# Zero rows, a placement table, warm-up products and moved loads in a kernel of linear attention followed by two dense layers

## The chip, the cores and the metric

The kernel runs on one core of a Trainium2 chip. The metric is the device time of one execution in microseconds (us). Times are given as the median over the runs of a kernel, with the lowest and highest in brackets. Where a profile is read, "span" is the profiled core's time from first to last recorded work, a little shorter than the device time.

## The reference

```python
# q, k, v, o_gate: (4, 8, 768, 40); i_gate, f_gate: (4, 8, 768)
for t in range(S):
    m_new = np.maximum(f_gate[:, :, t] + m, i_gate[:, :, t])
    f_stab = np.exp(f_gate[:, :, t] + m - m_new)
    i_stab = np.exp(i_gate[:, :, t] - m_new)
    C = f_stab * C + i_stab * outer(v_t, k_t)          # 40 x 40 state
    n = f_stab * n + i_stab * k_t
    y[t] = sigmoid(o_gate[t]) * (C @ q_t) / np.maximum(np.abs(n @ q_t), 1.0)
x = y.transpose(0, 2, 1, 3).reshape(3072, 320)
h = np.maximum(x @ w_in, 0.0)                            # w_in: 320 x 2048
out = (s * (h * h) + b) @ w_out                          # w_out: 2048 x 320
```

With gates as large as these, only the first 42 time steps still weigh in the state at later times. The kernel uses 42 rows of k and v for each head, checks on the chip that this was allowed (the "flag" steps), and holds a full version that isn't run with these inputs.

## The kernel before

The 3072 tokens go through in six chunks of 512. A chunk has four rounds of products for the two dense layers, and the attention of the *next* chunk is spread over sixteen slots between them, 0 to 15. Chunks 0 to 3 hold most of one batch each. Chunks 4 and 5 hold the first and last 128 tokens of every batch and need more steps.

```python
# one chunk, in the order in which PE gets its work
at = self.events(c + 1) if c + 1 < 6 else {}
for k in range(4):
    self.mm1_rem(c, k, 0); self.mm1_rem(c, k, 1)       # remainder products, 64 rows
    for a in range(2):
        self.mm1(c, k, a)                              # main products of layer 1
        self.square(*prev)                             # VectorE, of the half round before
        self.relu(c, k, a)                             # ScalarE
        for n, (f0, f1) in enumerate((((0, 3), (3, 6)), ((6, 11), (11, 16)))[a]):
            for e in at.get(4 * k + 2 * a + n, []):    # slot
                e()
            self.mm2(c - 1, k, f0, f1)                 # layer 2 of the chunk before
```

The attention operands have 42 rows, and one transpose buffer in PSUM (`psT`, one deep) serves nearly every attention step:

```python
self.kp = c.tile([L, B, 9, D], BF16, name="kp")        # L = 42
self.v1 = c.tile([L, B, 9, D + 1], BF16, name="v1")
self.psT = ctx.enter_context(tc.tile_pool(name="psT", bufs=1, space=PSUM))
...
def ev_vr(self, bb):
    ps = self.psT.tile([3 * L, 3, 3, D + 1], F32, tag="t", name="ps_vr")
    for g in range(3):
        nc.tensor.matmul(ps[:, g, :, :], lhsT=self.sel..., rhs=self.v1[:, bb, 3 * g : 3 * g + 3, :], ...)
    nc.vector.tensor_tensor(out=vbd, in0=ps, in1=self.bdl..., op=ALU.mult)
```

`ev_q` transposes the queries (`ps_q`), `ev_cn` builds the state (`ps_cn`), `ev_h` multiplies queries by state (`ps_h`) and starts a chain of five VectorE operations that ends in `x`. `ev_x` transposes `x` (`ps_x`) into the input `xt` of the layers. `ev_kt` and `ev_vr` make `kbd` and `vbd` for chunks 4 and 5, `ev_s` makes scores (`ps_s`) and `pm`. `warm(n)` issues n products of ones that nobody reads. They keep the matrix engine's clock up.

## Time and profile before

| kernel before | value |
|---|---|
| median of 3 runs | 161.21 us (161.01 to 161.81) |
| profiled run | 161.73 us, span 160.0 us, mean granted clock 0.972 |
| PE / VectorE / ScalarE busy | 89% / 55% / 49% of the span |

PE is the matrix engine, DVE is VectorE, ACT is ScalarE. The list of waits of PE gives the engine and tile, what ended the wait, the total in us, the number of times and the longest one:

```profile
PE o L424 <- DVE osb L430: 2.9, 3, 1.0
PE hp L380 <- ACT xt L366: 2.9, 3, 1.1
PE ps_q L290 <- ACT qb L275: 1.9, 2, 0.9
```

The first and the third line are holes in chunks 1, 3 and 4, where PE is the bound: 4.8 us that a better placement could close. The second stands in chunk 0 and at the opening of chunk 1, where products of the first layer wait for their transposed input.

### The profile page before, as it was taken

Reading aid. Unit: us, or ns where it says so; the run is one execution under the profiler, and the core shown is the slowest. Engines: PE = TensorE matmul, PEld = TensorE weight load, DVE = VectorE, ACT = ScalarE, POOL = GpSimd, SP = SyncE. Lnnn points to the kernel's source line nnn. Section 1 sums busy time; section 2 is a strip of 40 time slices with the busy share of each in tenths; the row PEclk is TensorE's granted clock in tenths of the full one; section 3 lists DMA queues with packets and bytes.
Section 4 is the critical chain, followed back from the end, with each engine's and each line's share of the span. In section 5 each row is a group of like instructions: output and inputs, shape, how many; then the busy total and the mean of one; then the engine's idle time right before and its main releaser. Section 6 shows DMA issues by size and latency. Waiting matters only on the chain.

```text
span 160.0 us, 2702 instructions
## 1 busy us (share of the span) xinstructions
PE 141.6 (89%) x1053; PEld 83.1 (52%) x1067; DVE 88.6 (55%) x188; ACT 78.7 (49%) x92; POOL 20.4 (13%) x48
## 2 busy tenths in 40 slices
PE   7896799889999799999979997979998899999970
PEld 7674443346555445665445563535544554556750
DVE  1486379951496665867436668335695444344220
ACT  4242468735674548855484454474725543533000
POOL 7974975000000000000000000000000000000000
PEclk9998589999999999999999999999999999999997
DMA  3999999920590110169501049610010111110221
GB/s 70 313 173 272 248 169 167 310 85 0 148 259 9 41 41 2 49 134 194 124 0 45 0 99 198 117 41 26 15 43 4 41 41 41 41 45 11 78 82 53
DMA packets 32265, 15.32 MB, mean 96 GB/s; under 512 B 20596, under 2 KB 31668, under 8 KB 32244
## 3 DMA queue, kind: packets, MB, share of 16 engines
q1 hardware_dynamic: 27000, 9.71, 25.0%
q0 software_dynamic: 4544, 5.24, 16.3%
q8 instruction: 10, 0.16, 0.5%
q10 hardware_dynamic: 700, 0.11, 0.4%
q14 instruction: 11, 0.09, 0.2%
HBM read 13.75 MB, written 3.93 MB: 110 GB/s over the span
## 4 chain that ended last, share of the span: by engine, by line
PE 62%; DVE 13%; DMA 10%; ACT 4%; issue 4%; POOL 4%; POOLq 0%; DVEq 0%; ACTq 0%
PE o L424 22%; PE hp L392 21%; DMA wi<-in_moe_w_in_dram 9%; PE o2t L424 5%; PE hp L380 5%; DVE fac L347 3%; DVE x L352 3%; PE ps_q L290 2%; DVE osb L430 2%; ACT xt L366 2%; PE ps_h L324 2%; ACT r L399 1%; PE ps_b L412 1%; PE ps_x L364 1%; DMA out_dram<-osb 1%
## 5 line engine op out<-in xcount | busy, mean ns | idle before, releaser
L399 ACT ACTIVATE r<-hp 128x1024 bf16<-128x1024 f32 x48 | 49.2, 1024 | 56.8 <-PE hp L392 56.0
L424 PE MATMUL o<-wo,g 128*128 128x320 bf16 x320 | 53.0, 299 | 3.2 <-DVE osb L430 2.9
L392 PE MATMUL hp<-xt,wi 128*128 128x512 bf16 (+1 forms) x186 | 48.1, 379 | 1.7 <-issue 1.1
L424 PEld LDWEIGHTS <-g 128*128 128x128 bf16 x384 | 35.5, 98 | 19.4 <-issue 4.5
L406 DVE TENSOR_TENSOR g<-r 128x1024 bf16<-128x1024 bf16 x48 | 32.1, 682 | 9.4 <-ACT r L399 9.3
L392 PEld LDWEIGHTS <-wi 128*128 128x128 bf16 x200 | 17.4, 99 | 23.7 <-issue 10.4
L430 DVE SCALAR_TENSOR_TENSOR osb<-o,sc,brep 128x320 f32<-128x320 f32 x20 | 11.0, 548 | 16.4 <-PE o L424 16.3
L380 PE MATMUL hp<-xt,wr 64*128 64x512 bf16 (+1 forms) x100 | 16.4, 382 | 3.3 <-ACT xt L366 2.9
L366 ACT COPY xt<-ps_x 128x768 bf16<-128x768 bf16 x12 | 9.5, 794 | 5.0 <-PE ps_x L364 5.0
L347 DVE SCALAR_TENSOR_TENSOR fac<-th,rec 128x640 f32<-128x640 f32 x12 | 9.9, 824 | 0.6
L352 DVE TENSOR_TENSOR x<-ps_h,fac 128x640 bf16<-128x640 f32 x12 | 9.9, 824 | 0.4
L380 PEld LDWEIGHTS <-wr 64*128 64x128 bf16 x100 | 3.9, 95 | 9.9 <-issue 7.9
L424 PE MATMUL o2t<-wo,g 128*128 128x320 bf16 x64 | 8.9, 299 | 0.0
L490 PE MATMUL ps_w<-ones 128*128 128x128 bf16 x96 | 7.8, 249 | 1.1 <-POOL ones L131 1.1
L290 PE MATMUL ps_q<-idb,qb 128*128 128x128 bf16 x72 | 6.2, 227 | 2.7 <-ACT qb L275 1.9
L290 PEld LDWEIGHTS <-qb 128*128 128x128 bf16 x72 | 5.0, 102 | 5.0 <-ACT qb L275 2.6
L490 PEld LDWEIGHTS <-ones 128*128 128x128 bf16 x96 | 7.0, 115 | 1.2 <-POOL ones L131 1.1
L293 ACT COPY qt<-ps_q 128x768 bf16<-128x768 bf16 x9 | 7.2, 797 | 0.6 <-PE ps_q L290 0.6
L364 PE MATMUL ps_x<-idb,x 128*128 128x128 bf16 x72 | 6.6, 227 | 0.8 <-DVE x L352 0.2
L364 PEld LDWEIGHTS <-x 128*128 128x128 bf16 x72 | 5.2, 102 | 4.0 <-DVE x L352 1.3
L281 ACT ACTIVATE th<-ox 128x640 f32<-128x640 f32 x8 | 5.8, 733 | 0.3 <-DMA ox<-in_o_gate_dram 0.3
L430 DVE SCALAR_TENSOR_TENSOR osb<-o2t,sc,brep 128x320 f32<-128x320 f32 x4 | 2.2, 550 | 5.9 <-PE o2t L424 5.9
(90 smaller groups left out, 88.0 us busy)
## 6 DMA issues: line engine op xcount, KB each, us to landing
out_dram<-osb SPq DMA_DIRECT2D x24, 160.0 KB, 2.4
qx<-in_q_dram SPq DMA_DIRECT2D x2, 640.0 KB
ox<-in_o_gate_dram SPq DMA_DIRECT2D x2, 640.0 KB
qx<-in_q_dram POOLq DMA_DIRECT2D x2, 640.0 KB, 9.9
ox<-in_o_gate_dram POOLq DMA_DIRECT2D x2, 640.0 KB, 10.9
wo<-in_moe_w_out_dram POOLq DMA_DIRECT2D x4, 320.0 KB, 7.0
qy<-in_q_dram SPq DMA_DIRECT2D x8, 160.0 KB, 3.2
oy<-in_o_gate_dram SPq DMA_DIRECT2D x8, 160.0 KB, 3.7
```

The lines of the kernel that those rows point to most:

```text
L290: nc.tensor.transpose(ps[:, j, g, :], self.qb[:, t0 + j, g * 120 : g * 120 + P], self.idb[:])
L347: nc.vector.scalar_tensor_tensor(out=fac, in0=self.th.pop((c, i))[:, :, :, :].rearrange("p j h d -> p (j h) d"), scalar=1.0, in1=rec[:, :] ...
L352: nc.vector.tensor_tensor(out=x[:, :, 0:DM].rearrange("p j (h d) -> p j h d", h=H), in0=hv[:, :, :, 0:D], in1=fac[:, :, :].rearrange("p (j ...
L364: nc.tensor.transpose(ps[:, j, kt, :], x[:, j, kt * P : (kt + 1) * P], self.idb[:])
L366: nc.scalar.copy(out=self.xt[:, :, t0 : t0 + 2 * P].rearrange("p k (j t) -> p j k t", j=2), in_=ps)
L380: nc.tensor.matmul(hp[:, e, n0:n1], lhsT=self.wr[64 * e : 64 * e + 64, k, a * P : (a + 1) * P], rhs=self.xt[64 * e : 64 * e + 64, 2, t0 + ...
L392: nc.tensor.matmul(hp[:, e, n0:n1], lhsT=self.wi[:, kt, f * P : (f + 1) * P], rhs=self.xt[:, kt, t0 + n0 : t0 + n1], start=False, stop=(kt ...
L399: self.nc.scalar.activation(out=r1, in_=self.hp.pop((c, k, a)), func=ACT.Relu)
L406: self.nc.vector.tensor_tensor(out=self.g[c][:, f : f + 3 : 2, :], in0=r1, in1=r1, op=ALU.mult)
L424: nc.tensor.matmul(self.o2[c, tb][:], lhsT=self.g[c][:, f, tb * P : (tb + 1) * P], rhs=self.wo[:, f, :], start=(f == 0), stop=(f == NF - 1),)
L430: nc.vector.scalar_tensor_tensor(out=osb, in0=self.o2.pop((c, tb)), scalar=self.sc[:, 0:1], in1=self.brep, op0=ALU.mult, op1=ALU.add)
L490: self.nc.tensor.matmul(self.ps_w[:, 0:P], lhsT=self.ones[:], rhs=self.ones[:], start=True, stop=True)
```

## The change

Its intent is to make PE's small products as cheap as large ones, to hold PE's clock during the start, and to put every attention step where PE doesn't wait for it. Cut to its core:

```diff
-        self.kp = c.tile([L, B, 9, D], BF16, name="kp")
-        nc.gpsimd.memset(self.kp[:, :, 8, :], 0.0)
+        self.kp = c.tile([P, B, 9, D], BF16, name="kp")        # P = 128
+        nc.vector.memset(self.kp, 0.0)
+        self.v1 = c.tile([P, B, 9, D + 1], BF16, name="v1")
+        nc.vector.memset(self.v1, 0.0)
...  # tri42, sel, ps_kt likewise; kbd, vbd 2 -> 4 buffers, r1 3 -> 4
-        self.warm(6)
+        self.warm(10)
...  # 12 -> 16, 8 -> 12, 36 -> 40, and two new warm(14) in chunk 0
+    def load_rest2(self):                                       # fa, ia: now after k, v; issued in chunk 1
...
-    def events(self, c):
+    def events(self):
+        put(0, 3, self.ev_q, 1, 1, v)                           # before: slot 4
+        put(0, 4, self.ev_h, 1, 0)                              # 5
+        put(0, 8, self.ev_x, 1, 0)                              # 9
+        put(0, 8, self.ev_h, 1, 1)                              # 10
+        put(0, 12, self.ev_x, 1, 1)                             # 14
+        put(0, 13, self.make_tri)                               # 11
+        # chunk 1: (q0, t0, e0, h0, q1, t1, e1, x0, h1, x1)
+        (3, 4, 5, 8, 5, 8, 7, 10, 12, 14)
+        put(1, 6, self.ev_kt, 0); put(1, 9, self.ev_vr, 0)      # before: all eight
+        put(1, 11, self.ev_kt, 1); put(1, 13, self.ev_vr, 1)    #   ps_kt and ps_vr
+        put(2, 12, self.ev_kt, 2); put(2, 13, self.ev_vr, 2)    #   in chunks 3 and 4
+        put(2, 14, self.ev_kt, 3); put(2, 15, self.ev_vr, 3)
+        for c in (4, 5):                                        # d = c - 1
+            put(d - 1, 13, self.qcast, c, 0, a)                 # a chunk earlier
...  # flag steps from chunks 1 and 2 to 2 and 3; loads of y about eight slots earlier
-            nc.sync.dma_start(out=dst, in_=osb)
+            eng = nc.scalar if (c, tb) == (5, CT - 1) else nc.sync
+            eng.dma_start(out=dst, in_=osb)
```

More of the change, by code (lines that the diff above doesn't have):

```diff
@@ L86, in load_rest @@
         nc.sync.dma_start(out=self.bc, in_=d["b"].partition_broadcast(P))
+        self.load_kv(2, B, nc.sync)
+    def load_rest2(self):
+        nc, d = self.nc, self.d
         nc.sync.dma_start(out=self.fa, in_=d["f"].rearrange("b h (a s) -> (b h a) s", a=4))
         nc.sync.dma_start(out=self.ia, in_=d["i"].rearrange("b h (a s) -> (b h a) s", a=4))
-        self.load_kv(2, B, nc.sync)
     def load_kv(self, b0, b1, eng):
@@ L148, in masks @@
             )
-        self.kp = c.tile([L, B, 9, D], BF16, name="kp")
-        nc.gpsimd.memset(self.kp[:, :, 8, :], 0.0)
-        self.v1 = c.tile([L, B, 9, D + 1], BF16, name="v1")
-        nc.gpsimd.memset(self.v1[:, :, 0:H, D : D + 1], 1.0)
-        nc.gpsimd.memset(self.v1[:, :, H, :], 0.0)
+        self.kp = c.tile([P, B, 9, D], BF16, name="kp")
+        nc.vector.memset(self.kp, 0.0)
+        self.v1 = c.tile([P, B, 9, D + 1], BF16, name="v1")
+        nc.vector.memset(self.v1, 0.0)
+        nc.gpsimd.memset(self.v1[0:L, :, 0:H, D : D + 1], 1.0)
         self.qb = c.tile([P, 6 * CT, 368], BF16, name="qb")
@@ L161, in masks_late @@
         nc, c = self.nc, self.const
-        self.tri42 = c.tile([L, P], BF16, name="tri42")
+        self.tri42 = c.tile([P, P], BF16, name="tri42")
         nc.gpsimd.memset(self.tri42, 1.0)
@@ L167, in masks_late @@
         )
-        self.sel = c.tile([L, 3, L], BF16, name="sel")
-        nc.gpsimd.tensor_copy(out=self.sel, in_=self.idb[0:L, 0:L].unsqueeze(1).to_broadcast([L, 3, L]))
+        self.sel = c.tile([P, 3, L], BF16, name="sel")
+        nc.gpsimd.tensor_copy(out=self.sel, in_=self.idb[:, 0:L].unsqueeze(1).to_broadcast([P, 3, L]))
         nc.gpsimd.memset(self.ib2[:, :, 1:2], 2.0)
@@ L207, in kw @@
         nc.vector.tensor_tensor(
-            out=self.kp[:, bb, 0:H, :],
+            out=self.kp[0:L, bb, 0:H, :],
             in0=self.k32[:, bb * H : (bb + 1) * H, :],
@@ L214, in vw @@
     def vw(self, bb):
-        self.nc.gpsimd.tensor_copy(out=self.v1[:, bb, 0:H, 0:D], in_=self.v32[:, bb * H : (bb + 1) * H, :])
+        self.nc.gpsimd.tensor_copy(out=self.v1[0:L, bb, 0:H, 0:D], in_=self.v32[:, bb * H : (bb + 1) * H, :])
     def ev_cn(self, bb):
@@ L233, in ev_kt @@
         nc = self.nc
-        ps = self.psT.tile([3 * D, 3, L], BF16, tag="t", name="ps_kt")
+        ps = self.psT.tile([3 * D, 3, P], BF16, tag="t", name="ps_kt")
         for g in range(3):
             nc.tensor.transpose(
-                ps[:, g, :], self.kp[:, bb, 3 * g : 3 * g + 3, :].rearrange("k a m -> k (a m)"), self.idb[0:L, 0:L]
+                ps[:, g, :], self.kp[:, bb, 3 * g : 3 * g + 3, :].rearrange("k a m -> k (a m)"), self.idb[:]
             )
-        kbd = self.kbd[bb] = self.work.tile([3 * D, 3, 3, L], BF16, tag="kbd", bufs=2, name="kbd")
+        kbd = self.kbd[bb] = self.work.tile([3 * D, 3, 3, L], BF16, tag="kbd", bufs=B, name="kbd")
         nc.vector.tensor_tensor(
             out=kbd,
-            in0=ps[:, :, :].unsqueeze(2).to_broadcast([3 * D, 3, 3, L]),
+            in0=ps[:, :, 0:L].unsqueeze(2).to_broadcast([3 * D, 3, 3, L]),
             in1=self.bdm[0 : 3 * D, :].unsqueeze(1).unsqueeze(3).to_broadcast([3 * D, 3, 3, L]),
@@ L254, in ev_vr @@
             )
-        vbd = self.vbd[bb] = self.work.tile([3 * L, 3, 3, D + 1], BF16, tag="vbd", bufs=2, name="vbd")
+        vbd = self.vbd[bb] = self.work.tile([3 * L, 3, 3, D + 1], BF16, tag="vbd", bufs=B, name="vbd")
         nc.vector.tensor_tensor(
@@ L397, in relu @@
     def relu(self, c, k, a):
-        r1 = self.r1[c, k, a] = self.work.tile([P, 2, N], BF16, tag="r1", name="r1")
+        r1 = self.r1[c, k, a] = self.work.tile([P, 2, N], BF16, tag="r1", bufs=4, name="r1")
         self.nc.scalar.activation(out=r1, in_=self.hp.pop((c, k, a)), func=ACT.Relu)
@@ L490, in warm @@
             self.nc.tensor.matmul(self.ps_w[:, 0:P], lhsT=self.ones[:], rhs=self.ones[:], start=True, stop=True)
-    def events(self, c):
-        if c == 1:
-            return {
-                0: [lambda: self.kw(1), lambda: self.qcast(1, 0, self.nc.vector)], 1: [lambda: self.ev_cn(1)],
-                2: [lambda: self.ev_q(1, 0, self.nc.vector), lambda: self.qcast(1, 1, self.nc.vector)],
-                3: [lambda: self.tanh(1, 0)], 4: [lambda: self.ev_q(1, 1, self.nc.vector)],
-                5: [lambda: self.ev_h(1, 0)], 6: [lambda: self.tanh(1, 1)], 9: [lambda: self.ev_x(1, 0)],
-                10: [lambda: self.ev_h(1, 1)], 14: [lambda: self.ev_x(1, 1)],
-            }
-        e = {}
-        def put(at, *steps):
-            for n, step in zip(at, steps):
-                e.setdefault(n, []).append(step)
-        late = 2 if c == 2 else 0
-        for i in range(2):
-            n = late + 3 * i
-            put((n, n + 1), lambda i=i: self.qcast(c, i, self.nc.scalar), lambda i=i: self.tanh(c, i))
-        if c < B:
-            put(
-                (0, 1, 2 + late, 4 + late, 5 + late, 8 + late, 9 + late, 13 + late // 2), lambda: self.kw(c),
-                lambda: self.ev_cn(c), lambda: self.ev_q(c, 0), lambda: self.ev_h(c, 0), lambda: self.ev_q(c, 1),
-                lambda: self.ev_x(c, 0), lambda: self.ev_h(c, 1), lambda: self.ev_x(c, 1),
-            )
-            return e
-        for i, at in enumerate(((0, 1, 3, 4, 6, 10), (2, 5, 7, 8, 11, 14))):
-            bb, _ = self.pair(c, i)
-            put(
-                at, lambda bb=bb: self.ev_kt(bb), lambda i=i: self.ev_q(c, i), lambda bb=bb: self.ev_vr(bb),
-                lambda i=i: self.ev_s(c, i), lambda i=i: self.ev_h(c, i), lambda i=i: self.ev_x(c, i),
-            )
@@ new lines, in events, with put @@
+    def events(self):
+        e = {}
+        def put(c, at, step, *args):
+            e.setdefault((c, at), []).append(lambda: step(*args))
+        v, a = self.nc.vector, self.nc.scalar
+        put(0, 0, self.kw, 1)
+        put(0, 0, self.qcast, 1, 0, v)
+        put(0, 1, self.ev_cn, 1)
+        put(0, 1, self.qcast, 1, 1, v)
+        put(0, 2, self.ev_q, 1, 0, v)
+        put(0, 3, self.tanh, 1, 0)
+        put(0, 3, self.ev_q, 1, 1, v)
+        put(0, 4, self.ev_h, 1, 0)
+        put(0, 5, self.tanh, 1, 1)
+        put(0, 8, self.ev_x, 1, 0)
+        put(0, 8, self.ev_h, 1, 1)
+        put(0, 12, self.ev_x, 1, 1)
+        put(0, 13, self.make_tri)
+        put(1, 3, self.bias)
+        put(1, 3, self.load_rest2)
+        for c in (2, 3):
+            q0, t0, e0, h0, q1, t1, e1, x0, h1, x1 = (
+                (3, 4, 5, 8, 5, 8, 7, 10, 12, 14) if c == 2 else (0, 1, 2, 4, 3, 4, 5, 7, 8, 11)
+            )
+            d = c - 1
+            put(d, 0, self.kw, c)
+            put(d, 1, self.ev_cn, c)
+            put(d, q0, self.qcast, c, 0, a)
+            put(d, t0, self.tanh, c, 0)
+            put(d, e0, self.ev_q, c, 0)
+            put(d, h0, self.ev_h, c, 0)
+            put(d, q1, self.qcast, c, 1, a)
+            put(d, t1, self.tanh, c, 1)
+            put(d, e1, self.ev_q, c, 1)
+            put(d, x0, self.ev_x, c, 0)
+            put(d, h1, self.ev_h, c, 1)
+            put(d, x1, self.ev_x, c, 1)
+        put(1, 6, self.ev_kt, 0)
+        put(1, 9, self.ev_vr, 0)
+        put(1, 11, self.ev_kt, 1)
+        put(1, 13, self.ev_vr, 1)
+        put(2, 12, self.ev_kt, 2)
+        put(2, 13, self.ev_vr, 2)
+        put(2, 14, self.ev_kt, 3)
+        put(2, 15, self.ev_vr, 3)
+        for c in (4, 5):
+            d = c - 1
+            put(d - 1, 13, self.qcast, c, 0, a)
+            put(d, 0, self.ev_q, c, 0)
+            put(d, 1, self.qcast, c, 1, a)
+            put(d, 1, self.tanh, c, 0)
+            put(d, 2, self.ev_s, c, 0)
+            put(d, 3, self.ev_q, c, 1)
+            put(d, 3, self.tanh, c, 1)
+            put(d, 4, self.ev_h, c, 0)
+            put(d, 5, self.ev_s, c, 1)
+            put(d, 7, self.ev_x, c, 0)
+            put(d, 8, self.ev_h, c, 1)
+            put(d, 11, self.ev_x, c, 1)
+        put(1, 4, self.load_x, 3, self.nc.sync)
+        put(1, 15, self.load_y, 0, self.nc.sync)
+        put(2, 15, self.load_y, 2, self.nc.sync)
+        put(2, 1, self.flag_a)
+        put(2, 5, self.flag_b)
+        put(2, 9, self.flag_c)
+        put(3, 9, self.flag_d)
@@ L553, in start @@
         self.qcast(0, 1, nc.scalar)
-        self.warm(12)
+        self.warm(16)
         self.ev_q(0, 0)
         self.ev_q(0, 1, nc.vector, early=True)
-        self.warm(8)
+        self.warm(12)
         self.tanh(0, 0)
@@ L561, in start @@
         self.ev_h(0, 1, early=True)
-        self.warm(36)
+        self.warm(40)
         self.ev_x(0, 0)
+        self.warm(14)
     def run(self):
@@ L569, in run @@
             prev = None
-            extra = {
-                (0, 2): self.make_tri, (1, 0): lambda: self.load_x(3, nc.sync), (1, 1): self.flag_a,
-                (1, 2): self.flag_b, (1, 3): self.flag_c, (2, 0): self.flag_d,
-                (2, 1): lambda: self.load_y(0, nc.sync), (3, 1): lambda: self.load_y(2, nc.sync),
-            }
+            at = self.events()
             for c in range(6):
-                at = self.events(c + 1) if c + 1 < 6 else {}
                 for k in range(4):
@@ L586, in run @@
                         self.ev_x(0, 1)
+                        self.warm(14)
                     for a in range(2):
@@ L598, in run @@
                         for n, (f0, f1) in enumerate((((0, 3), (3, 6)), ((6, 11), (11, 16)))[a]):
-                            for e in at.get(4 * k + 2 * a + n, []):
+                            for e in at.pop((c, 4 * k + 2 * a + n), []):
                                 e()
-                            if c == 1 and k == 0 and a == 1 and n == 1:
-                                self.bias()
                             if c > 0:
                                 self.mm2(c - 1, k, f0, f1)
-                    if (c, k) in extra:
-                        extra[c, k]()
                 if c == 3:
                     self.asked = nc.values_load(self.flag[0:1, 0:1], min_val=0, max_val=1)
+            assert not at
             self.square(*prev)
```

## The prediction

> **What bounds the kernel now.** I read the share rows first, then the granted clock by slices, the list of waits, and the timeline of the matrix engine with its neighbours. A "chunk" below is one of six passes of 512 tokens. A chunk has four rounds. In a round the matrix engine (PE) runs 4 remainder products and 4 main products into the first layer's buffer, slot, 3 output products, slot, 3 output products, 4 main products, slot, 5 output products, slot, 5 output products. The attention of a later chunk is put into these sixteen slots, numbered 0 to 15.
>
> ```profile
> PE   7896799889999799999979997979998899999970
> DVE  1486379951496665867436668335695444344220
> PEclk9998589999999999999999999999999999999997
> ...
> 14.00:15.00 1.00, 0.82 (x6) 0.61 (x7) 0.71 (x3) 0.00 (x0) 0.00 (x0) 0.80 1.06 326
> 15.00:16.00 1.00, 0.91 (x8) 0.68 (x7) 0.00 (x0) 0.05 (x1) 0.00 (x0) 0.50 1.07 307
> ...
> 21.00:22.00 1.00, 0.69 (x5) 0.40 (x5) 1.00 (x3) 0.64 (x2) 0.70 (x2) 0.79 1.12 152
> ```
>
> PE is full from 33 us on: that is the bound of chunks 1 to 5. Before that the granted clock is half (0.50) between about 14.6 and 21.4 us. But there PE is not what decides, as the timeline shows:
>
> ```profile
> 18.51 0.59 DVE L277 CAST qb<-qx 128x640 bf16<-128x640 f32 x1 [3.77 <-DMA qx<-in_q_dram]
> ...
> 32.58 0.61 PE L380 MATMUL hp<-xt,wr 64*128 64x512 bf16 x4 [1.08 <-ACT xt L366]
> ...
> 53.09 0.97 PE L424 MATMUL o<-wo,g 128*128 128x320 bf16 x6 [0.97 <-DVE osb L430]
> ...
> 81.02 0.51 PE L290 MATMUL ps_q<-idb,qb 128*128 128x128 bf16 x6 [0.95 <-ACT qb L275]
> ...
> 99.36 0.97 PE L424 MATMUL o<-wo,g 128*128 128x320 bf16 x6 [0.97 <-DVE osb L430]
> ```
>
> VectorE (DVE) waits 3.77 us for the queries of batch 1 and then works almost without a pause from 18.51 to 32.7 us; chunk 1 opens at 32.58 when the last transposed input is copied. Later PE has holes of 0.95 us: at 53.1, 81.0, 99.4, and the same again at 106.3 and 124.6. From first remainder product to the next chunk's, chunks 1 to 5 take 24.6, 20.5, 25.3, 25.2 and 18.1 us; the last has no attention in it. A tail of 8.7 us of output products and about 5 us to the end follow.
>
> **What the Trainium skill says.** "TensorE: Matmul & The Clock Gate", Part 1, says that the array falls to half rate after an idle window of about 3.4 us and comes back after a busy one. The trace agrees: the low stretch is 6.8 us, two windows, and the window before it was busy about 2.0 of 3.4 us (59%). The same page, under LDWEIGHTS, says that a load of 32 rows takes as long as one of 128, so zero rows cost PE nothing. "VectorE: DVE Perf Modes", Zero memsets can be issued as uint32, says one cycle per element, at the 0.96 GHz of its Specifications. No DVE memset is in this trace; 640 elements in 0.82 us (L347) fit that order.
>
> **The change part by part.** *Zero rows.* The trace has the price of 42 rows:
>
> ```profile
> 83.79 0.38 PE L251 MATMUL ps_vr<-v,sel 42*126 42x123 bf16 x3
> 84.10 0.85 PE L424 MATMUL o<-wo,g 128*128 128x320 bf16 x5
> ...
> 111.57 0.34 PE L302 MATMUL ps_s<-qt,kbd 120*126 120x128 bf16 x3
> 111.75 0.57 PE L424 MATMUL o<-wo,g 128*128 128x320 bf16 x3
> ```
>
> Start to start, three products of 42 rows take 0.31 us, three of 120 rows 0.18; the work before a 42-row group is also 0.1 us too long (5 output products in 0.79 instead of 0.68). So about 0.2 us each for two ps_cn, four ps_kt and four ps_vr on the full stretch: 10 x 0.2 = 2.0 us saved. The two new DVE memsets are 720 words and 1476 elements, an estimate of 2.3 us by that page; from 0.8 us they end near 3.2. The gate scan then starts 0.8 us later, but its exponent was ready at 3.98 and PE took it at 4.62 after its warm-up, so this is hidden.
>
> *Warm-up.* Four more warm-up products (0.057 us each, 0.23 us) fit into holes of 0.35, 0.33, 0.11 and 0.25 us; 14 more (0.8 us) fit the two holes of 0.89. PE then stays at full clock to about 17 us. But v of batch 1 still comes at about 18.2 and q at 18.5.
>
> *The table, chunk 0.* The instruction order has both ps_q of batch 1 in a row, in one PSUM buffer, and DVE puts cast, cn, cast and a square ahead of the first copy. From 18.45: casts and cn 1.75, square 0.68, copy 0.55, so the second ps_q starts near 21.5 and PE idles 2.0 us in the 3.4 before. By the 59% case the clock should fall there. At full clock ps_h follows at 23.1 and its chain begins at 23.7 (before: 23.11); at half clock at 25.5. Then 2.6 chain, two squares 1.3, 2.4 chain: x ready at 30.0 to 31.8. In the new order ps_x, then ps_tri behind the copy of xt (1.6), then a round half (1.1), its relu (1.2) and the remainder (0.4) come in series: main products of chunk 1 at 34.3 to 36.1, before 33.1. **+1.2 to +3.0 us, +2 taken.**
>
> *The table, chunks 1 to 4.* Without waits a chunk is 18.1 plus attention, start to start: q, x 0.34 each, ps_h 0.31, cn, kt, vr, s 0.19 each, bias 2.17, flags 0.45. Waits follow from this chain:
>
> ```profile
> 88.88 0.32 PE L324 MATMUL ps_h<-vbd,pm 126*128 126x123 bf16 x3
> ...
> 91.03 0.82 DVE L352 TENSOR_TENSOR x<-ps_h,fac 128x640 bf16<-128x640 f32 x1
> 91.89 0.19 DVE L356 COPY x<-x 128x128 bf16<-128x128 bf16 x1
> 92.00 0.54 DVE L256 TENSOR_TENSOR vbd<-ps_vr,bdl 126x369 bf16<-126x369 f32 x1
> ```
>
> x is ready 3.0 us after ps_h is issued, and a vbd queued behind it frees the transpose buffer at 3.7.
> Chunk 1: 18.1 + 2.17 + 0.19 + 4x0.34 + 2x0.31 + 4x0.19 = 23.2. ps_h in slot 8 and ps_x in slot 10 are 2.15 us apart on PE, so PE waits 3.7 - 2.15 = 1.55, again at 12 and 14. ps_kt in slot 6 waits 0.7 for relu, tanh and copy on ACT, then 0.1; in slot 11 0.4 for xt. Sum 4.3, and 0.15 lost in refilling after each of four: 28.1, **+3.5**.
> Chunk 2: 18.1 + 3.4 = 21.5; ps_x behind the flag reductions 0.75, ps_vr behind kbd 0.4, 0.1, refill 0.3: 23.0, **+2.5**.
> Chunks 3 and 4: 18.1 + 1.36 + 0.62 + 0.38 = 20.45; in slot 7 ps_x waits for a pm queued behind the chain 0.87, in slot 11 0.35, 0.1, refill 0.3: 22.1, **-3.2 and -3.1**. The osb and cast holes of before go.
> Chunk 5, tail and the last store on another queue: 0. Sum: 2 + 3.5 + 2.5 - 6.3 = **+1.7 us**, or 162.9.
>
> **The rivals.** *R1, the placement works:* the new holes are overlapped. Then chunks 1 to 4 are 23.2 + 21.5 + 20.45 + 20.45 = 85.6 against 95.6, and the time falls by up to 10 us; with half of the new holes closed and chunk 0 level, about 156. For it: DVE is only 55% busy, and the holes it aims at are real. Against: the transpose buffer is still single, and its next user stands behind a 2.6 us chain. *R2, a trade:* chunks 3 and 4 gain what 1 and 2 lose, 160 to 163. *R3, the clock:* the low stretch moves to where it delays the chain of batch 1, and lasts two windows; 164 to 165. For it: the 2 us hole; against: the window's phase is free, so it varies by run.
>
> **Range and chances.** R2 is my sum. My waits take every PE arrival at its earliest, and a delay upstream shortens the waits downstream, so I take about 2 us off the 8 us of new waits: 161.0 us. R1 stretches the range down to 157.0, R3 up to 164.5. Faster by over 2% needs under 158.0, over half of the new holes gone: 0.22. Slower needs over 164.4: 0.13. Same: 0.65.
>
> **What would show it.** Right: 42-row groups gone and their successors 0.2 us sooner; holes near 1.5 us before two ps_x of chunk 1; no 0.95 us holes in chunks 3 and 4, now about 22 us; clock full to 17 us and a low stretch after 18; ps_tri waiting for xt. Wrong: chunk 1 starting before 32 us, or chunks 1 and 2 no longer than 25 and 21.

## The result, and the profile after

| | before | after |
|---|---|---|
| median, runs of one job | 161.32 us (161.01 to 161.81), 4 runs | 159.69 us (159.55 to 159.84), 4 runs |
| profiled run: span, clock | 160.0 us, 0.972 | 157.9 us, 0.991 |

The ratio is 0.9897, with a 95% interval of 0.9869 to 0.9924. Ratios here are the mean time of one kernel's fast runs over the mean of the other's fast runs of the same rounds, so not quite the ratio of the medians. The change is about 1% faster, which counts as the same at a threshold of 2%. The predicted 161.0 us was 1.3 us too high; the measurement lies in the range.

The share rows of the changed kernel's page (forty equal slices, tenths of full):

```profile
PE   7999799689896969999899979999899999999960
DVE  6477679752448577587674587635768334434220
PEclk9999999999999999999999999999999999999996
```

The low clock of slices 4 to 6 is gone. PE has two new dips in chunk 1 (slices 13 and 15). In the list of waits, with the columns of the list above, the old entries for `osb` and `qb` are gone, and these have come:

```profile
PE ps_x L368 <- DVE vbd L260: 2.6, 2, 1.3
PE ps_x L368 <- DVE pm L311: 1.4, 2, 0.7
```

This is the first of them in the timeline (start, duration, engine, line, operation, tiles, and in brackets the idle time before and what ended it):

```profile
46.65 0.47 PE L328 MATMUL ps_h<-cn,qt 120*128 120x123 bf16 x6
47.36 0.33 PE L255 MATMUL ps_vr<-v,sel 128*126 128x123 bf16 x3
47.53 0.57 PE L428 MATMUL o<-wo,g 128*128 128x320 bf16 x3
48.71 0.82 DVE L356 TENSOR_TENSOR x<-ps_h,fac 128x640 bf16<-128x640 f32 x1
49.68 0.54 DVE L260 TENSOR_TENSOR vbd<-ps_vr,bdl 126x369 bf16<-126x369 f32 x1
50.27 0.49 PE L368 MATMUL ps_x<-idb,x 128*128 128x128 bf16 x6 [1.31 <-DVE vbd L260]
```

`ps_vr` has filled the one transpose buffer. PE gets to `ps_x` at about 48.96 us. `x` itself ends at 49.53, so about 0.6 of the 1.31 us are a wait for `x`, as `ps_x` stands only two slots behind `ps_h`. The other 0.7 us are the buffer: the operation that empties it, `vbd`, stands on DVE behind the chain from `ps_h` to `x` and ends at 50.22. The same lines show the gain of the zero rows: three `ps_vr` products now take 0.17 us from start to start (47.36 to 47.53), where the prediction read 0.31.

Opening of chunk 1, the same view:

```profile
29.87 0.22 PE L203 MATMUL ps_tri<-tri,sel 128*126 128x128 bf16 x1 [0.89 <-ACT xt L370]
32.49 0.39 PE L384 MATMUL hp<-xt,wr 64*128 64x512 bf16 x2 [0.79 <-ACT r L403]
32.82 1.04 PE L396 MATMUL hp<-xt,wi 128*128 128x512 bf16 x4
```

Main products of chunk 1 start at 32.82 us, 0.3 us before those of the kernel before, instead of the predicted 34.3 to 36.1.

The next table cuts the spans by PE's timeline: to the first main product of chunk 1, from there to the first remainder product of chunk 2, then from chunk to chunk, to the start of the last output's scaling on DVE, and to the end. Three of its columns belong to experiments that are told below.

| stage, us | before | before, loads moved | before, zero rows + warm-up | after | last variant |
|---|---|---|---|---|---|
| granted clock in chunk 0 | half for 6.8 us | full | full | full | full |
| to main products of chunk 1 | 33.12 | 31.21 | 30.99 | 32.82 | 32.15 |
| chunk 1 | 24.06 | 24.07 | 23.82 | 26.60 | 22.86 |
| chunk 2 | 20.54 | 20.53 | 20.36 | 22.60 | 21.59 |
| chunk 3 | 25.28 | 25.29 | 24.95 | 21.90 | 21.24 |
| chunk 4 | 25.21 | 25.21 | 24.89 | 21.82 | 20.61 |
| chunk 5 to last output | 26.97 | 26.97 | 26.97 | 26.97 | 26.97 |
| last output to end | 4.82 | 4.82 | 5.02 | 5.19 | 5.18 |
| span | 160.0 | 158.1 | 157.0 | 157.9 | 150.6 |

From before to after, chunks 3 and 4 gave 6.8 us, and chunks 1 and 2 took 4.6 back. Why chunk 0 came out level could not be read from these two traces alone; it became the question of the experiments.

### The profile page after: what moved, and what is told of

Same layout as the page of the kernel before. It is cut to its first block, busy times and chain, and to the rows that moved or that the text cites. A ratio compares the mean times of both kernels' runs of the same rounds, so it can differ in the third digit from the quotient of the medians.

```text
span 157.9 us, 2789 instructions
## 1 busy us (share of the span) xinstructions
PE 140.4 (89%) x1097; PEld 84.7 (54%) x1111; DVE 90.9 (58%) x190; ACT 79.4 (50%) x92; POOL 20.0 (13%) x46
## 4 chain that ended last, share of the span: by engine, by line
PE 62%; DVE 18%; DMA 9%; ACT 3%; issue 3%; POOL 2%; DVEq 0%
PE o L428 21%; PE hp L396 19%; DMA wi<-in_moe_w_in_dram 9%; PE hp L384 7%; PE o2t L428 6%; DVE fac L351 5%; DVE x L356 5%; PE ps_x L368 3%; PE ps_h L328 2%; PE ps_q L294 2%; DVE rec L349 2%; PE ps_b L416 1%; ACT r L403 1%; DVE dd L345 1%; ACT xt L370 1%
## 5 line engine op out<-in xcount | busy, mean ns | idle before, releaser
L428 PE MATMUL o<-wo,g 128*128 128x320 bf16 x320 | 53.6, 299 | 0.0
L396 PE MATMUL hp<-xt,wi 128*128 128x512 bf16 (+1 forms) x186 | 46.8, 371 | 1.7 <-issue 1.3
L410 DVE TENSOR_TENSOR g<-r 128x1024 bf16<-128x1024 bf16 x48 | 32.9, 689 | 14.1 <-ACT r L403 14.0
L396 PEld LDWEIGHTS <-wi 128*128 128x128 bf16 x200 | 17.1, 98 | 22.6 <-issue 9.6
L384 PE MATMUL hp<-xt,wr 64*128 64x512 bf16 (+1 forms) x100 | 15.8, 374 | 1.3 <-ACT r L403 0.8
L495 PE MATMUL ps_w<-ones 128*128 128x128 bf16 x140 | 10.7, 242 | 1.1 <-POOL ones L134 1.1
L495 PEld LDWEIGHTS <-ones 128*128 128x128 bf16 x140 | 9.7, 110 | 1.1 <-POOL ones L134 1.1
L368 PEld LDWEIGHTS <-x 128*128 128x128 bf16 x72 | 4.5, 97 | 9.4 <-DVE x L356 5.4
```

The source lines that it names most:

```text
L368: nc.tensor.transpose(ps[:, j, kt, :], x[:, j, kt * P : (kt + 1) * P], self.idb[:])
L384: nc.tensor.matmul(hp[:, e, n0:n1], lhsT=self.wr[64 * e : 64 * e + 64, k, a * P : (a + 1) * P], rhs=self.xt[64 * e : 64 * e + 64, 2, t0 + ...
L396: nc.tensor.matmul(hp[:, e, n0:n1], lhsT=self.wi[:, kt, f * P : (f + 1) * P], rhs=self.xt[:, kt, t0 + n0 : t0 + n1], start=False, stop=(kt ...
L410: self.nc.vector.tensor_tensor(out=self.g[c][:, f : f + 3 : 2, :], in0=r1, in1=r1, op=ALU.mult)
L428: nc.tensor.matmul(self.o2[c, tb][:], lhsT=self.g[c][:, f, tb * P : (tb + 1) * P], rhs=self.wo[:, f, :], start=(f == 0), stop=(f == NF - 1),)
L495: self.nc.tensor.matmul(self.ps_w[:, 0:P], lhsT=self.ones[:], rhs=self.ones[:], start=True, stop=True)
```

## The experiments

Twelve kernels ran, in three jobs of four with five rounds each. All gave correct results, and all ratios are against the kernel before in the same job. A run more than 1.5% above the fastest of its kernel counts as slow and is left out of the ratios. There were four: one of the kernel before, one of a variant in the second job and two of a variant in the third. The medians and brackets below list all runs. The two clock groups that are told next lie within the fast runs, since the rule goes by time and not by clock.

### First job: the parts alone

My theory was that the placement is a trade and the zero rows are the gain. The rivals were that the warm-up products, through the clock, or the order of loads, through the queries, had brought it.

**Zero rows alone** in the kernel before (with the two memsets on DVE).

```diff
-        self.kp = c.tile([L, B, 9, D], BF16, name="kp")
+        self.kp = c.tile([P, B, 9, D], BF16, name="kp")     # and v1, tri42, sel, ps_kt; zeroed on DVE
```

> The kernel before, with the zero rows alone (placement, warm-up and load order of before). Theory: each 42-row group on the full stretch (2 ps_cn, 4 ps_kt, 4 ps_vr) gets 0.2 us shorter and nothing eats it: about 2.0 us less than before, 159.3 us, with ps_vr at about 0.18 us start to start instead of 0.31. Rival: the holes behind casts and osb only grow by what PE gains: under 0.7 us less.

**Warm-up products alone** in the kernel before.

```diff
-        self.warm(6)
+        self.warm(10)        # 12 -> 16, 8 -> 12, 36 -> 40; + two warm(14)
```

> The kernel before, with the additional warm-up products alone. Theory: the granted clock stays at 1.00 past 14.6 us, but chunk 0 is set by the landing of the queries of batch 1 and the VectorE work behind it, so the main products of chunk 1 still start near 33 us: between 0 and 0.7 us less. Rival (the half clock held chunk 0 up): 1.5 us less or more.

**Order of the early loads alone** in the kernel before: the large gate loads after k and v.

```diff
+        self.load_kv(2, B, nc.sync)
         nc.sync.dma_start(out=self.fa, ...)
         nc.sync.dma_start(out=self.ia, ...)
-        self.load_kv(2, B, nc.sync)
```

> The kernel before, with the gate loads fa and ia issued after k and v of batches 2 and 3 instead of ahead of them, and nothing else. Theory: the queries of batch 1 land about 1.5 us sooner (before 18.5, after the change 16.8) because less traffic stands in their way; chunk 1 opens 0.5 to 1.5 us sooner, as PE at half clock then becomes what VectorE waits for. Rival: the sooner landing came from the earlier issue on the GpSimd queue or is noise: landing at 18.3 to 18.5, time the same within 0.3 us.

**The changed kernel with the loads of before.**

```diff
-        self.load_kv(2, B, nc.sync)       # first
-        put(1, 3, self.load_rest2)        # fa, ia late
+        # fa, ia, then load_kv(2, B), as before
```

> The changed kernel with the load order of before. Theory: the queries of batch 1 land near 18.5 again, PE's hole before the second ps_q grows from 1.05 to about 2 us, and chunk 1 opens 1.5 us later, or up to 3 us later if the clock falls in that hole: 161.2 to 162.7 us. Rival: landing unchanged at 16.8, 159.7 us.

| kernel | median, us | ratio, 95% |
|---|---|---|
| before + zero rows | 159.85 (158.41 to 160.60) | 0.9906 (0.9840 to 0.9972) |
| before + warm-up | 160.36 (160.18 to 161.50) | 0.9950 (0.9895 to 1.0005) |
| before + moved loads | 160.70 (159.85 to 161.85) | 0.9994 (0.9928 to 1.0061) |
| after, loads back | 160.15 (159.77 to 160.41) | 0.9943 (0.9888 to 0.9998) |

The list of single runs told more than the medians. The kernel before fell into two groups: six runs at 160.06 to 161.01 us with a mean granted clock of 0.991 to 0.997, and five at 161.75 to 161.99 with 0.972 to 0.985. Zero rows and moved loads alone split the same way: 158.41 to 159.38 against 160.32 to 160.60, and 159.85 to 160.15 against 161.26 to 161.85. Their two profiles happened to fall in different groups. First zero rows alone, then moved loads alone, the row of the granted clock:

```profile
PEclk9998579999999999999999999999999999999999
```

```profile
PEclk9999999999999999999999999999999999999997
```

The profile with full clock is the second column of tables above. From chunk 1 on it equals the kernel before within 0.01 us in every chunk; its chunk 1 opens 1.91 us earlier:

```profile
31.21 1.04 PE L392 MATMUL hp<-xt,wi 128*128 128x512 bf16 x4
```

Not all of the 1.91 us is the clock. The queries of batch 1 were cast at 18.51 us in the trace of before and at 17.83 in this one, so 0.68 us lay ahead of the cast. From the cast to the main products of chunk 1 it took 14.6 us at half clock (15.1 in the profile of zero rows alone) and 13.4 at full clock (13.5 and 13.6 in two profiles below, 64 rows and zero rows with warm-up). So half clock cost 1.0 to 1.7 us on this path. The traces show the place: at half clock DVE waits for PE before it can copy the first `ps_q`. First the kernel before, then moved loads alone:

```profile
20.63 0.56 DVE L295 COPY qt<-ps_q 128x768 bf16<-128x768 bf16 x1 [0.48 <-PE ps_q L290]
```

```profile
19.29 0.55 DVE L295 COPY qt<-ps_q 128x768 bf16<-128x768 bf16 x1
```

The copy starts 2.12 us after the start of the cast in the first and 1.46 us after it in the second. Whether an execution of the kernel before runs at half clock there varies from run to run. Over all three jobs, 32 of its 33 runs were fast: 11 of them had a clock of 0.985 or less (161.39 to 161.99 us, median 161.77), and 21 had 0.991 or more (159.61 to 161.18, median 160.22). The profile on which the prediction rested was one of the first kind.

Like with like, zero rows are worth 1.1 us at full clock (median 159.08 against 160.22) and 1.4 at low clock (160.34 against 161.77); against the runs of their own job alone it is 1.0 and 1.6. That lies between the theory (2.0) and the rival (under 0.7).

The warm-up products make no execution that runs at full clock faster. They take away the slow group: all seven of their runs had a clock of 0.991 or more, although one of them took 161.50 us. That one is the profiled run, and its trace shows the reason: its sixteen warm-up products before the first `ps_q` took 1.89 us, against 1.05 in the profile of zero rows with warm-up, and its first `ps_x` came at 13.69 us instead of 11.6. Until about 10 us PE did 12 products in a microsecond, later 22. The column of the granted clock says 1.00 all the same, so it doesn't vouch for the first microseconds. The gain of the warm-up shifts the mean only.

The order of loads moves nothing beyond the noise, and both expectations about it missed: alone it brought the cast to 17.83 us (theory about 17, rival 18.3 to 18.5), and the old order in the changed kernel gave a cast at 17.15 and not near 18.5, and 160.15 us and not 161.2 or more. Putting it back in the changed kernel costs 0.46 us between the medians, taken from two jobs, which I wouldn't build on.

### Second job: the placement

The theory was now that zero rows and warm-up together explain more than the whole gain, so that the new placement costs time; the rival was that some gain needed the new placement. From here on, times of different jobs are also compared. The full-clock runs of the kernel before had medians of 160.12, 160.65 and 160.22 us in the three jobs, so such a difference can be off by half a microsecond.

**Zero rows and warm-up** in the kernel before: both edits above.

> The kernel before, with zero rows and additional warm-up, but its own placement and load order. Seen so far: the kernel before has two times, near 160.1 us at full clock and near 161.9 us where the clock falls to half in chunk 0; zero rows alone took 1.2 to 1.5 us off in either; the warm-up alone left only the first time, 160.2. Theory (the two parts add, and the new placement as a whole costs time): 159.0 us in all executions, 0.5 to 0.8 us less than the changed kernel. Rival (the placement is worth something once both are there): 159.7 us or more.

**The changed kernel with 42 rows.**

```diff
-        self.kp = c.tile([P, B, 9, D], BF16, name="kp")
+        self.kp = c.tile([L, B, 9, D], BF16, name="kp")     # and v1, tri42, sel, ps_kt, memsets as before
```

> The changed kernel with 42-row operands again. Theory: 0.2 us for each of ten groups come back on the full stretch, less where a wait follows: 1.2 to 2.0 us more than the changed kernel, 161.0 to 161.7 us. Rival (the new waits swallow them): under 0.7 us more.

**The changed kernel with chunk 0 placed as before.**

```diff
-        put(0, 3, self.ev_q, 1, 1, v)
-        put(0, 4, self.ev_h, 1, 0)
-        put(0, 8, self.ev_x, 1, 0)
-        put(0, 8, self.ev_h, 1, 1)
-        put(0, 12, self.ev_x, 1, 1)
-        put(0, 13, self.make_tri)
+        put(0, 4, self.ev_q, 1, 1, v)      # second cast: slot 2; tanh: 6
+        put(0, 5, self.ev_h, 1, 0)
+        put(0, 9, self.ev_x, 1, 0)
+        put(0, 10, self.ev_h, 1, 1)
+        put(0, 11, self.make_tri)
+        put(0, 14, self.ev_x, 1, 1)
```

> The changed kernel with the steps of chunk 0 in the slots they had before (second ps_q in slot 4, last ps_x in slot 14, ps_tri in slot 11). Theory: ps_tri no longer stands between the last ps_x and the last products of chunk 0 and the second ps_q no longer waits for a copy: main products of chunk 1 start 1.2 to 1.8 us sooner than 33.0, so 157.9 to 158.5 us. Rival (chunk 1 cannot use it, as its queries land late): 159.4 us or more.

**The changed kernel with the attention of chunk 2 early in chunk 1, and ps_kt and ps_vr behind it.**

```diff
-   (3, 4, 5, 8, 5, 8, 7, 10, 12, 14)
+   (2, 3, 3, 4, 3, 4, 5, 7, 8, 11)
-   put(1, 6, self.ev_kt, 0); put(1, 9, self.ev_vr, 0); put(1, 11, self.ev_kt, 1); put(1, 13, self.ev_vr, 1)
+   put(1, 12, self.ev_kt, 0); put(1, 13, self.ev_vr, 0); put(1, 14, self.ev_kt, 1); put(1, 15, self.ev_vr, 1)
```

> The changed kernel with the attention of batch 2 in chunk 1 placed as that of batch 3 in chunk 2 (ps_h in slots 4 and 8, ps_x in 7 and 11), and kt and vr in slots 12 to 15. Theory: the two waits of 1.31 us before ps_x and those of 0.41 and 0.21 go, one of about 0.25 comes at ps_vr: chunk 1 falls from 28.1 to about 25 us, total 156.2 to 157.0 us. Rival (the queries of batch 2 land too late for it): a wait of over 1 us at the cast or tanh of batch 2, total 158.5 us or more.

| kernel | median, us | ratio, 95% |
|---|---|---|
| before + zero rows + warm-up | 158.68 (158.37 to 159.23) | 0.9861 (0.9820 to 0.9902) |
| after, 42 rows | 161.03 (160.76 to 162.81) | 1.0003 (0.9963 to 1.0044) |
| after, chunk 0 placed as before | 158.08 (157.81 to 158.40) | 0.9820 (0.9782 to 0.9859) |
| after, attention early in chunk 1 | 157.05 (156.92 to 159.89) | 0.9759 (0.9721 to 0.9797) |

Zero rows and warm-up in the old placement take 158.68 us (159.0 was expected), 1.0 less than the whole change. The rest of the change therefore costs about 1 us net. In the table of stages, the third column against the fourth: chunk 0 +1.83, chunk 1 +2.78, chunk 2 +2.24, chunks 3 and 4 -3.05 and -3.07, the last store +0.17, together +0.9. With 42 rows the changed kernel is 0.4 us slower than the full-clock runs of the kernel before in the same job (161.03 against 160.65), which points the same way; the zero rows are worth 1.3 us in it (161.03 less 159.69, from two jobs).

Chunk 0 as before is worth 1.6 us (159.69 less 158.08). Its main products of chunk 1 start at 31.00 us instead of 32.82. The eight moved steps were put back together, so which of them costs how much stays open. The early attention in chunk 1 is worth 2.6 us (157.05, where 156.2 to 157.0 was expected), and both holes of 1.31 us were gone from its profile, as the theory had it. This edit does two things at once, which weren't tried apart: `ps_x` follows `ps_h` by three slots and not two, and `ps_kt` and `ps_vr` stand behind both.

That profile fell in the one run of seven that took 159.89 us, a slow one that doesn't count in the ratio. It is shown only for what the clock did. The columns are the stretch in us, its slow-down, PE, PE loads, DVE, ACT and POOL busy (instructions), the granted clock, DMA share and GB/s:

```profile
28.00:29.00 1.00, 0.33 (x4) 0.22 (x5) 0.96 (x3) 0.97 (x1) 0.00 (x0) 1.00 1.07 355
29.00:30.00 1.00, 0.30 (x4) 0.22 (x4) 1.00 (x2) 0.67 (x1) 0.00 (x0) 1.00 1.11 339
...
32.00:33.00 1.00, 0.64 (x3) 0.13 (x3) 0.00 (x0) 0.87 (x1) 0.00 (x0) 0.50 0.14 45
```

PE is busy for a third of two microseconds while it waits for `x` and `xt` at the end of chunk 0, in idle times of 0.89 us at most. Shortly after, the clock drops to half, from about 31.2 to 38.0 us.

The third rival of the prediction put such a fall behind the hole before the second `ps_q` of chunk 0. There it is in the profile of the changed kernel with 42 rows, the run of 162.81 us at a mean clock of 0.980:

```profile
20.52 0.49 PE L294 MATMUL ps_q<-idb,qb 128*128 128x128 bf16 x6 [1.40 <-DVE qt L299]
```

```profile
22.00:23.00 1.00, 1.00 (x6) 0.45 (x5) 0.20 (x1) 0.01 (x1) 1.00 (x2) 0.50 1.32 185
```

Its queries were cast at 17.91 us, the clock was half from about 21.5 to 24.9 us, and the main products of chunk 1 started at 34.61 us. Both kernels have the added warm-up products, which therefore make a fall rarer and don't exclude it. In the changed kernel itself no run showed one: its clock was 0.991 or more in all four runs.

### Third job: do the gains add, and two open causes

**Both placement edits at once** in the changed kernel: the last two diffs together.

> After, with both of the slot changes that were tried alone: chunk 0 in the slots of before (158.08) and the attention of chunk 1 early, with ps_kt and ps_vr behind it (157.05). Theory: each was worth something in another chunk, so the gains add: 157.05 less the 1.6 us of chunk 0 is 155.4 us, 155.0 to 155.9; in the profile chunk 1 opens near 30.5 us and the two 1.31 us holes of ps_x in it are gone. Rival: the gains overlap, because the queries of batch 2, landing near 31 us, are too late for an early cast once chunk 1 opens sooner: 156.5 us or more, with a PE hole before the first ps_q of chunk 1.

**All PE waits of the changed kernel moved out of the way.** On top of the two edits:

```diff
-   put(1, 3, self.bias)
+   put(0, 15, self.bias)                      # beside the copy of xt
-   put(0, 11, self.make_tri)
+   put(1, 0, self.make_tri)
+   # ps_kt 0..3: (1,12) (1,15) (2,12) (2,15);  ps_vr 0..3: (1,14) (2,0) (2,14) (3,14)
-   put(d, 7, self.ev_x, c, 0);  put(d, 11, self.ev_x, c, 1)
+   put(d, 8, self.ev_x, c, 0);  put(d, 12, self.ev_x, c, 1)
-   put(2, 9, self.flag_c);  put(3, 9, self.flag_d)
+   put(3, 10, self.flag_c); put(3, 13, self.flag_d)
```

> The kernel above with the other PE waits of the profile of after moved out of the way: bias to slot 15 of chunk 0 and ps_tri to slot 0 of chunk 1 (so that the wait of 0.9 us for the copy of xt has work beside it), one ps_kt or ps_vr to a slot at the end of a chunk, ps_x of chunks 3 and 4 one slot later (holes of 0.72 and 0.64 us behind pm), the flag reductions of DVE away from ps_x (0.33 us). Theory: the holes of a PE-bound stretch add up: 155.4 less 0.9, 0.3, 0.3 and 1.4, with 0.7 for refilling, is about 151.8 us; 151.3 to 153. Rival: a moved step only finds the next wait, since one buffer and one 2.6 us chain serve all of it: 154 us or more, with new holes of like size.

**64 rows instead of 128**, in the kernel before.

```diff
-        self.kp = c.tile([L, B, 9, D], BF16, name="kp")
+        self.kp = c.tile([64, B, 9, D], BF16, name="kp")    # and v1, tri42, sel, ps_kt; zeroed on DVE
```

> Before with the attention operands padded to 64 rows instead of 42, not to 128. Tells what of the 0.13 us a group is: the row count, or that a group of part height stands among products of full height. Theory (the switch between part and full height): 64 rows cost as 42 do: ps_vr 0.31 us start to start, time as before in each of its two clock states (about 160.1 and 161.8). Rival (only 42, not a whole quarter of the array, is slow): ps_vr 0.18 us as with 128 rows, 158.4 to 159.1 us at full clock, 160.3 to 160.6 at low.

**The changed kernel without the added warm-up products.**

```diff
-        self.warm(10)
+        self.warm(6)         # 16 -> 12, 12 -> 8, 40 -> 36; both warm(14) removed
```

> After without the added warm-up products, all else kept. Theory: the warm-ups act through the granted clock alone: in some of the executions the clock falls to half in chunk 0 again, seen as a mean clock under 0.985, and those take 1 to 2 us longer (160.7 to 161.8); the others stay near 159.7. Rival: the other parts already hold the clock, so nothing changes (159.5 to 160.0 in all executions, clock over 0.99).

| kernel | median, us | ratio, 95% |
|---|---|---|
| after, both placement edits | 155.17 (154.36 to 155.41) | 0.9663 (0.9618 to 0.9708) |
| after, all waits moved | 152.24 (151.85 to 153.07) | 0.9489 (0.9444 to 0.9535) |
| before, 64 rows | 160.25 (159.97 to 161.76) | 1.0013 (0.9960 to 1.0066) |
| after, warm-up as before | 160.27 (159.50 to 162.81) | 0.9963 (0.9905 to 1.0021) |

The gains add: 157.05 less 1.6 was expected at 155.4, and 155.17 was measured. The last variant was expected at 151.8 (151.3 to 153) and took 152.24. It is faster than both kernels: about 4% faster than the change, taken as the quotient of the two ratios. Its list of waits of PE now begins so:

```profile
PE ps_w L495 <- POOL ones L134: 1.1, 1, 1.1
PE ps_q L294 <- ACT qb L279: 1.1, 1, 1.1
PE ps_q L294 <- DVE qb L281: 0.5, 2, 0.3
```

No wait for `vbd`, `pm`, `xt` or the flags is left in that list. The 1.1 us before `ps_q` stand in chunk 1, behind a cast that ACT runs after a relu; that one could still be moved.

With 64 rows nothing is gained. `ps_vr` there, in the timeline:

```profile
82.04 0.38 PE L251 MATMUL ps_vr<-v,sel 64*126 64x123 bf16 x3
82.35 0.85 PE L424 MATMUL o<-wo,g 128*128 128x320 bf16 x5
```

The three products again take 0.31 us from start to start, as with 42 rows. The step lies between 64 rows and all 128. The record of weight loads (PEld) shows where the time goes. First 64 rows, then the changed kernel with 128:

```profile
82.04 0.24 PEld L251 LDWEIGHTS <-sel 64*126 64x126 bf16 x3 [0.26 <-issue]
```

```profile
80.82 0.45 PEld L255 LDWEIGHTS <-sel 128*126 128x126 bf16 x3
```

The loads of 64 rows begin only with their products, at 82.04 us, and the loader stood idle before. Those of 128 rows begin 0.26 us ahead of their products (81.08 us), while the products before them still run. Why the loads of part height don't run ahead, no run shows.

Without the added warm-up, four runs of the changed kernel took 159.50 to 160.32 us at a clock of 0.990 or more, and two took 162.59 and 162.81 at 0.959 and 0.958. These two are slow by the rule and not in the ratio. That some executions have a low clock again fits the theory and not the rival; the size of their delay (over the 1 to 2 us expected) is not read from slow runs, and the profile fell in the first group, so where the clock fell is not known. Over all runs of the three jobs and of the change, 2 of 55 with the added warm-up had a mean clock of 0.985 or less, and 21 of 57 without it. The four fast runs lie within 0.6 us of the change's own time, as the theory had it for full clock.

## Why the prediction was right or wrong

**The total.** 161.0 us were predicted and 159.69 measured, inside 157.0 to 164.5, and "within 2%" was the right class. The picture of the second rival, a trade, was right as well. The correction of 2 us for delays was right in kind: 8.2 us of new waits in chunks 1 to 4 were worked out and 5.2 measured. With it these chunks come out right, -2.3 us against -2.2. What is left of the error is chunk 0, by 2.3 us.

**"But there PE is not what decides" was the wrong step.** The sentence said of half clock in chunk 0 that it costs nothing, since DVE waits for the queries then. The kernel's own runs refute it: 160.22 us at full and 161.77 at low clock, and from the cast to chunk 1 it took 14.6 us at half clock and 13.4 at full. The wait of 0.48 us of DVE for `ps_q` stood in the prediction's own trace, in the stretch that it calls "almost without a pause". I had one profile, took its chunk 0 for the kernel's chunk 0, and worked out the change's chunk 0 against it. The prediction used "the window's phase is free" for the new kernel, as a reason for a spread, and not for the old one, whose three runs of 161.0 to 161.8 us looked like one state.

**Chunk 0, "+1.2 to +3.0, +2 taken".** Against a full-clock execution the new placement does cost that: 32.82 against 30.99 us is +1.8, and putting the old slots back returned 1.6. Against the low-clock profile it was -0.3, so the sum held +2 where -0.3 was measured. The chain that the prediction followed was right: it has 15.85 us at full clock from the cast to the main products (18.45 to 34.3), and the trace has 15.99 (16.06 and 15.78 in two other profiles with the new slots at full clock). What failed is its start, "q at 18.5", and the middle that was taken between full and half clock: 1.5 and 0.8 of the 2.3 us. The low stretch after 18 us did not come in the changed kernel. The queries were cast from 16.83 and not from 18.45 us, and a cast took 0.49 instead of 0.59 us:

```profile
16.83 0.49 DVE L281 CAST qb<-qx 128x640 bf16<-128x640 f32 x1 [1.89 <-DMA qx<-in_q_dram]
18.95 0.55 DVE L299 COPY qt<-ps_q 128x768 bf16<-128x768 bf16 x1
19.56 0.49 PE L294 MATMUL ps_q<-idb,qb 128*128 128x128 bf16 x6 [1.04 <-DVE qt L299]
```

The second `ps_q` came at 19.56 instead of 21.5, with 1.04 us of idle time instead of 2.0. Why the queries landed sooner is in part open. POOL (GpSimd) issued their load at 8.46 instead of 8.94 us; the profiles with zeroed rows have 8.45 to 8.61 there and those with 42 rows 8.68 to 8.98, since zeroing on DVE takes memsets off POOL. The other 1.2 us lie between issue and cast. Over all profiles the cast came between 16.8 and 18.5 us, and with the loads of before at 17.15.

**Chunk 1, 28.1 us.** The page seems to agree exactly, as 28.11 us lie between the first remainder products (31.31 and 59.42). But the first of these comes early there and its partner waits for a relu. Measured from the main products and with 0.54 us for four remainder products, chunk 1 took 27.1. The mechanism was right and its size 1.1 us too large: 1.55 us were predicted for each of the `ps_x` waits and 0.7, 0.1 and 0.4 for the rest, 4.3 in all, and 1.31, 1.31, 0.41 and 0.21 were measured, 3.24 in all.

**Chunks 2, 3 and 4.** Predicted 23.0, 22.1 and 22.1 us, measured 22.6, 21.9 and 21.8. In chunk 2 the waits were 0.33 us behind the flags and 0.23 behind `kbd`, where 0.75, 0.4 and 0.1 stood. The holes for `osb` and `qb` went, and `ps_x` waits for `pm` as predicted (0.87 expected, 0.72 and 0.64 measured). The second wait for `pm`, 0.35, did not occur in either chunk.

**Zero rows, "10 x 0.2 = 2.0 us saved".** The price of a group was right, but the sum is 1.1 to 1.4 us on the chip in the old placement. Waits there took some of it: the two holes before `ps_q` grew from 0.95 to 1.15 and 1.16 us, as PE came sooner to a thing that ACT delivers when it does, and one of 0.20 us came before a `ps_s`. In the table of stages the four chunks gain 0.25, 0.17, 0.34 and 0.32.

**The memsets** are hidden, as predicted. An estimate of 2.3 us stood for both; they took 1.95:

```profile
1.02 0.66 DVE L154 MEMSET kp<- 128x720 uint32 x1 [1.02 <-PEq L848]
1.94 1.29 DVE L156 MEMSET v<- 128x1476 bf16 x1 [0.26 <-issue]
```

**The last store, "0".** From the last scaling to the end it took 4.82 to 5.02 us in six profiles with the old queue (SyncE's), and 5.00 to 5.51 in eight with the new one (ScalarE's); the means are 4.89 and 5.25. This wasn't tried by itself, so that the queue is the cause is argued and not shown.

**The sum of the profile** in the prediction's terms: chunk 0 -0.3 instead of +2, chunk 1 +2.5 instead of +3.5, chunk 2 +2.1 instead of +2.5, chunks 3 and 4 -6.8 instead of -6.3, the end +0.4 instead of 0. That is -2.1 us, where +1.7 was worked out and -0.2 (161.21 to 161.0) was the value after a correction for delays. Most of the -2.1 is the state of this one profile of before, with half clock in chunk 0 and queries that landed late. With the full-clock runs of before as base, the mean gain of the change is 0.7 us (160.41 less 159.70, from different jobs). Its two near variants show none against full-clock runs of their own jobs: 160.15 against 160.12 us with the loads back, and 160.06 (fast runs) against 160.22 without the added warm-up.

**The first rival, "by up to 10 us".** Its floor for chunks 1 to 4 was 85.6 us. The last variant has 86.8 between the first remainder products of chunks 1 and 5 (31.61 and 118.45), but it does the 2.17 us of `bias` in chunk 0, so that its floor is 83.4. Most of the gain was there, and the table of this change kept it from coming out: it put `ps_x` close behind `ps_h` and moved `ps_vr` into the stretch between them, where the one buffer is needed.

## What to carry to other kernels

Before a profile is taken as the base of a prediction, list the mean granted clock of every run of that kernel: with runs in two clock groups, one profile shows one of them, and a change that only makes the good one likelier looks like a gain of work. A placement pays when no step takes a single buffer between the producer of a long chain and its consumer, and when the consumer stands far enough behind; move the buffer's other users behind the chain, one at a time, and the gains of separate holes add. Pad operands to full height only where the part-height groups stand on the bound engine's path, and pad to all rows, since half the rows gained nothing here.

## What the Trainium skill lacked or had wrong

- "TensorE: Matmul & The Clock Gate", LDWEIGHTS, and the row on small-K matmuls in "Why this matters for your kernels", say that 32 rows take the time of 128. One load agrees (131 ns for 42 rows in the profile of moved loads, 136 for 128 with zero rows and warm-up). In a stream it doesn't hold: three products of 42 or of 64 rows took 0.31 us from start to start, and 0.17 with 128 rows, and the kernel before gained 1.1 to 1.4 us by zero rows. The skill isn't silent on this: "TensorEngine Tiling (Array Packing)", Key Properties, says that changing the tiling mode drains the engine. Whether that is the cause here no run shows, and that page gives no time for it.
- The same page, Part 1, calls the window free-running and the ramp's penalty under 1% of a kernel. No run contradicts it: the fast runs of one and the same kernel took 160.22 us at full clock and 161.77 with a low stretch, which is 0.97%. But that is as much as the whole change measured, so at this size it can't be left out of a comparison.
- The same page, "Why this matters for your kernels", advises against idle gaps over about 3 us. In the kernel before the clock fell with no PE gap over 0.89 us, after 3.4 us in which PE was busy for about 59%; in two variants it fell after 53% (42 rows) and 52% (early attention). In the profile of moved loads it held, though PE was busy for only 59% in the least busy 3.4 us of its start too (12.8 to 16.2 us), and in the changed kernel it held with 65% or more. So no threshold follows. That frequent short idle times can make the clock fall the page says too, under "A second HAM failure mode"; it gives no busy share at which a window counts as idle.
- "VectorE: DVE Perf Modes", Zero memsets can be issued as uint32, says one cycle per element. Measured were 0.92 ns an element (720 words in 0.66 us) and 0.87 ns (1476 elements in 1.29 us), a little under the 1.04 ns of that page's 0.96 GHz.
